# Another order for one period of a recurrent-attention stage: scans a unit and a half ahead, state scan and router steps before the scaling of k, results turned back one period sooner

## The chip, the cores and the metric

The kernel runs on one core of a Trainium2 chip. The metric is the device time of one execution in microseconds; lower is better. Five engines work side by side, each through its own instruction queue in program order: PE (TensorE, matmuls and transposes into PSUM), DVE (VectorE), ACT (ScalarE), POOL (GpSimd) and SP (SyncE, which here issues loads). Instructions of different engines wait for each other through semaphores.

## What is computed

Three operators in a row, all in float32. First a recurrent attention over 4 batches, 8 heads, 768 tokens and 48 dimensions per head. Then a mixture of experts, where a router picks one of 8 experts for each of the 3072 rows. Then a dense feed-forward layer with a squared ReLU. The change touches the first operator and the router.

```python
for t in range(S):                                     # attention
    cur = einsum('bhd,bhe->bhde', u[None] * k_t, v_t)
    y[:, :, t] = einsum('bhd,bhde->bhe', r_t, state + cur)
    state = w_t[:, :, :, None] * state + einsum('bhd,bhe->bhde', k_t, v_t)
...
logits = x @ w_gate                                    # router
e_idx = argmax(logits, axis=1)
gate_w = softmax(logits)[arange(N), e_idx]
eom = sigmoid(x @ w_output_gate)
out[mask] = gate_w * eom * (relu(x[mask] @ w1[e]) @ w2[e])   # for every expert e
...
g = maximum(x @ w_in, 0.0) ** 2                        # dense layer
return g @ w_out
```

## The kernel before, in words

**Units.** The attention is cut into 16 units (`NU`), each one batch and two heads. A unit has 6 chunks of 128 tokens, and the chunks are worked in a parallel form: products inside a chunk, a state that is carried over the chunks, and products with that state. Class `Unit` (from L656) has one method for each stage. The stages of a unit, with the engine that carries each, are these.

- `w_turn` (PE, 6 transposes into two PSUM tiles `zw`), `w_check` (ACT, three instructions), `suffix` and `prefix` for the halves 0 and 1 (DVE: two running products `suf` and `ff` and a reciprocal for each half), `spread` (ACT, copies into `P`).
- `k_turn` and `r_turn`: 12 small transposes each on PE, then two DVE multiplications each, which write `kT` and `rA`. The text calls them the scaling of k and of r.
- `scores` for the halves 0 and 1: 12 matmuls on PE, two ACT copies into `A`, a mask on POOL (L741).
- `k_back` (12 transposes of `kT`, two ACT copies into `kP`), `states` (24 small matmuls), `state_scan` (DVE, writes `St`, L753).
- `gate_products` (POOL, L716 and L717), `gate_sum` (DVE, L721), `gate_values` (POOL, L724, writes `gv`), `bonus_in` (PE, 6 transposes of `gv` that open the output tiles `py`).
- `across` (20 matmuls with `St`) and `within` (24 matmuls with `A`), both adding into `py`; then two ACT copies of `py` into `xT`; `back` (12 transposes of `xT`, two ACT copies into the rows `xr`).

**The period.** The loop `for t in range(-1, NU + 1)` writes the program out by hand: one turn of it is a period, with stages of neighbouring units interleaved. Since every engine works in program order, the order of the calls in this loop is the order of the work on each engine. In period t the kernel before runs, in this order: scores half 0 of unit t, `back` of t-2, `bonus_in` of t-1, `w_turn` of t+2, `gate_sum` and `gate_values` of t, `w_check` of t+2, `k_back` of t, suffix half 0 of t+2, `k_turn` of t+1, `across` of t-1, `spread` of t+1, prefix half 0 of t+2, `r_turn` of t+1, scores half 1 of t, `gate_products` of t+1, suffix and prefix half 1 of t+2, `within` of t-1, `states` and `state_scan` of t.

**PSUM tiles.** `Ring` hands out four PSUM tiles in turn (three named `pt`, one `pa`) to all turns, scores, states and router steps. Each request reuses the tile of four requests before, and PE waits until that one has been read.

**The router's steps.** When the 4 units of a batch are done, `route_steps` (from L160) routes its 768 rows. It is a generator; each `yield` ends a step, and the table `PLAN` (for batches 0 and 1) or `LAST` (batch 2) says at which place of which period a step is issued. Step 1 is the logits on PE (12 matmuls of 256 columns, each issued as two) and an ACT copy `lt`; step 2 turns them back (`lg`); step 3 is the choice of the expert on DVE (L184 to L195, with an exponential `ez` on ACT); step 4 the second part (L198 to L204, with `sg` on ACT); then come the gate weights (L208 to L213), the two counting matmuls `pk` (L220, L221), the row numbers (L227 to L236), and six indirect stores of rows by POOL (L249), one step each.

**Behind the attention.** Batch 3 is routed while the first block of expert 0 (block A, rows of batches 0 to 2) is made ready: `rows_A`, `gather` (POOL), `scale` and `prep_x`, then `up(0)`, its first matmul (L348). `first_block_step` places these.

## Time and profile before

| | |
|---|---|
| median of 3 runs | 855.87 us (854.1 to 857.66) |
| the profiled execution | 851.45 us |
| its span, first to last instruction | 849.7 us |
| PE busy | 809.0 us (95%), 5868 matmuls |
| DVE busy | 532.1 us (63%) |
| ACT busy, POOL busy | 376.1 us (44%), 352.3 us (41%) |
| mean granted TensorE clock | 0.982 of full speed |

The span is one profiled execution; the 1.75 us around it belong to its time and not to the trace. "Busy" of PE counts overlapping records of pipelined matmuls, so 95% is not 95% of what PE can do. The attention lies between 0 and about 187 us; block A's first matmul starts at 190.47 us. In the timeline rows below, a bracket at the end of a row is the time its engine stood idle before it, and what it waited for.

### The profile page before, as it was taken

What the parts mean: (1) busy time and instruction counts of PE and PEld (TensorE: products, weight loads), DVE (VectorE), ACT (ScalarE), POOL (GpSimd) and SP (SyncE); (2) the same over time, 40 slices, a digit from 0 to 9 for tenths busy, and PEclk for the clock granted to TensorE, in tenths of its full rate; (3) what the DMA queues carried; (4) which work ended last, traced back from release to release, by engine and by line L of the source; (5) the groups of instructions that cost most, each with busy time, mean ns of one, the idle gap of its engine ahead of it and who ended that gap; (6) DMA issues with size and microseconds to landing.
All of it is one profiled execution on the core that took longest, in us unless ns stands there. A gap on an engine that the chain in (4) does not pass through costs nothing.

```text
span 849.7 us, 15473 instructions
## 1 busy us (share of the span) xinstructions
PE 809.0 (95%) x5868; PEld 732.2 (86%) x5868; DVE 532.1 (63%) x961; ACT 376.1 (44%) x789; POOL 352.3 (41%) x433
## 2 busy tenths in 40 slices
PE   5998989898899999999999999999999999999995
PEld 4887878778788999999999998888898999999994
DVE  7879787877367778777823688878633434434342
ACT  4565555552354454555544344343433333333321
POOL 6664766653345365455564233333211212123111
PEclk9899999999999999999999999999999999999998
DMA  9575565723596578477762231323204123032010
GB/s 199 112 140 117 138 125 125 222 80 133 132 201 200 172 210 237 130 247 210 169 192 80 79 114 53 128 75 111 75 1 140 31 82 112 2 109 76 1 47 37
DMA packets 157363, 102.89 MB, mean 121 GB/s; under 512 B 112348, under 2 KB 140940, under 8 KB 157284
## 3 DMA queue, kind: packets, MB, share of 16 engines
q1 hardware_dynamic: 149044, 86.55, 38.8%
q0 software_dynamic: 4912, 14.65, 5.0%
q10 hardware_dynamic: 3328, 0.66, 0.4%
q8 instruction: 47, 0.77, 0.4%
q14 instruction: 32, 0.26, 0.1%
HBM read 79.34 MB, written 22.50 MB: 120 GB/s over the span
## 4 chain that ended last, share of the span: by engine, by line
PE 58%; issue 12%; POOL 3%; another core or an unknown queue 0%; DVE 0%; ACT 0%; POOLq 0%; DVEq 0%; ACTq 0%
PE ph L348 10%; PE ph L349 10%; PE ph L350 10%; PE po L348 5%; PE po L350 5%; PE po L349 5%; PE px L350 5%; PE px L348 5%; PE px L349 4%; POOL out_dram L1186 2%; PE px L434 1%; PE po L434 0%; POOL x22l L343 0%; POOL x21l L343 0%; POOL x20l L343 0%
## 5 line engine op out<-in xcount | busy, mean ns | idle before, releaser
L1161 DVE SCALAR_TENSOR_TENSOR gg<-ph,rl 128x512 f32<-128x512 f32 x96 | 66.2, 689 | 121.8 <-ACT rl L1159 115.4
L1159 ACT ACTIVATE rl<-ph 128x512 f32<-128x512 f32 x96 | 57.4, 598 | 146.6 <-PE ph L350 135.5
L343 DVE TENSOR_TENSOR gl<-gg,gh 128x512 fp32r<-128x512 f32 x96 | 66.7, 695 | 65.9 <-ACT gh L341 39.2
L341 ACT CAST gh<-gg 128x512 fp32r<-128x512 f32 x96 | 59.6, 621 | 103.3 <-DVE gg L1161 103.3
L343 POOL TENSOR_TENSOR w1l<-w1r,w1h 128x384 fp32r<-128x384 f32 x56 | 59.5, 1067 | 67.0 <-ACT w1h L341 66.7
L337 ACT ACTIVATE hh<-ph 128x320 fp32r<-128x320 f32 (+7 forms) x64 | 32.4, 507 | 113.2 <-PE ph L350 106.0
L1107 POOL TENSOR_TENSOR caf<-caf,cbf 128x384 f32<-128x384 f32 x32 | 32.5, 1017 | 114.0 <-DVE cbf L1106 114.0
L343 DVE TENSOR_TENSOR w2l<-w2r,w2h 128x384 fp32r<-128x384 f32 x64 | 63.7, 998 | 20.1 <-ACT w2h L341 19.1
L338 DVE SCALAR_TENSOR_TENSOR hl<-ph,hh 128x320 fp32r<-128x320 f32 (+7 forms) x64 | 36.8, 575 | 37.1 <-ACT hh L337 33.0
L1186 POOL DMA_INDIRECT out_dram<-ob,tokc x24 | 23.4, 975 | 66.9 <-DVE ob L1184 64.8
L741 POOL TENSOR_SCALAR_AFFINE_SELECT A<-A 128x768 f32<-128x768 f32 x32 | 27.8, 868 | 45.4 <-ACT A L740 44.9
L348 PE MATMUL po<-hh,w2h 128*128 128x320 f32 (+4 forms) x120 | 42.3, 352 | 0.0
L349 PE MATMUL po<-hl,w2h 128*128 128x320 f32 (+4 forms) x120 | 41.4, 345 | 0.3 <-DVE hl L338 0.3
L350 PE MATMUL po<-hh,w2l 128*128 128x320 f32 (+4 forms) x120 | 41.2, 344 | 0.0
L343 POOL TENSOR_TENSOR x22l<-x2r,x22h 128x512 fp32r<-128x512 f32 x12 | 15.5, 1294 | 51.8 <-ACT x22h L341 51.8
L740 ACT COPY A<-pt 128x384 f32<-128x384 f32 x50 | 22.2, 482 | 32.6 <-PE pt L738 26.0
L738 PE MATMUL pt<-rA,kT 64*128 64x128 f32 x300 | 33.2, 304 | 2.0 <-DVE rA L711 1.4
L404 POOL DMA_INDIRECT xg<-x_rows,gi x28 | 29.0, 1035 | 14.9 <-DVE hl L338 8.5
L343 POOL TENSOR_TENSOR x21l<-x2r,x21h 128x512 fp32r<-128x512 f32 x12 | 15.5, 1291 | 45.5 <-ACT x21h L341 45.5
L341 ACT CAST w2h<-w2r 128x384 fp32r<-128x384 f32 x64 | 32.9, 516 | 0.0
L341 ACT CAST w1h<-w1r 128x384 fp32r<-128x384 f32 x64 | 32.6, 512 | 0.0
L249 POOL DMA_INDIRECT x_rows<-xr,dsi x24 | 24.4, 1018 | 18.8 <-DVE vals L242 14.8
(851 smaller groups left out, 2656.4 us busy)
## 6 DMA issues: line engine op xcount, KB each, us to landing
w1r<-in_moe_w_dram SPq DMA_DIRECT2D x16, 768.0 KB
w2r<-in_moe_w_dram SPq DMA_DIRECT2D x16, 768.0 KB
x2r<-x_cols SPq DMA_DIRECT2D x12, 768.0 KB
cq<-in_moe_w_in_dram SPq DMA_DIRECT2D x16, 384.0 KB
cq<-in_moe_w_out_dram SPq DMA_DIRECT2D x16, 384.0 KB
vN<-in_v_dram SPq DMA_DIRECT2D x32, 144.0 KB
part<-ob SPq DMA_DIRECT2D x24, 192.0 KB
ob<-part SPq DMA_DIRECT2D x24, 192.0 KB
```

Source lines behind the costliest of these rows:

```text
L337: nc.scalar.activation(hi, src, AF.Relu)
L338: nc.vector.scalar_tensor_tensor(lo, src, 0.0, hi.bitcast(F32), op0=ALU.max, op1=ALU.subtract)
L341: nc.scalar.copy(hi, src)
L343: lo_eng.tensor_tensor(lo, src, hi.bitcast(F32), op=ALU.subtract)
L348: nc.tensor.matmul(out_, a_of(ah), b_of(bh), start=start, stop=False)
L349: nc.tensor.matmul(out_, a_of(ah), b_of(bl), start=False, stop=False)
L350: nc.tensor.matmul(out_, a_of(al), b_of(bh), start=False, stop=stop)
L738: nc.tensor.matmul(pa[j][:, ci], self.kT[pp, hf * HC + ci], self.rA[pp, hf * HC + ci], start=True, stop=True)
L1107: nc.gpsimd.tensor_tensor(af, af, bf, op=ALU.add)
L1159: nc.scalar.activation(rl, ph, AF.Relu)
L1161: nc.vector.scalar_tensor_tensor(gg, ph, 0.0, rl, op0=ALU.max, op1=ALU.mult)
L1186: ins = nc.gpsimd.indirect_dma_start(out=out[:, :], out_offset=IndirectOffsetOnAxis(ap=tokc[:, n:n + 1], axis=0), in_=ob, in_offset=None)
```

## The change

It changes the order of one period, and little else. In period t the order is now: scores half 0 of unit t, `k_back` of t, `w_check` of t+2, `gate_products` of t+1, suffix and prefix half 1 of **t+1**, `within` of t-1, `states` and `state_scan` of t, the router's steps of the place "scan", scores half 1 of t, `spread` of t+1, `across` of t-1, `k_turn` and `r_turn` of t+1, `w_turn` of t+2, `bonus_in` of **t**, `gate_sum` and `gate_values` of **t+1**, suffix and prefix half 0 of t+2, and `back` of **t-1**. The scans thus run one and a half units ahead (before: two units), and only unit 0's first half is scanned before the loop. `within` stands before `across`, so the copies of `py` into `xT` follow `across`. The router's counting matmuls stand before the gate weights, with an ACT copy of their result for batches 0 to 2, and the steps have other places. Line numbers of the changed file are 4 smaller from there on.

```diff
 (route_steps)
-        if b < B - 1:
-            gate_weights()
-            yield
         pk = ps_t.tile([128, 512], F32, name=pn)
...
         nc.tensor.matmul(pkv[:, :, :NTB], upper[:, 0], oh, start=False, stop=True)
+        if b < B - 1:
+            nc.scalar.copy(inc, pkv)
+            pkv = inc
         yield
-        if b == B - 1:
-            gate_weights()
-            yield
+        nc.vector.tensor_reduce(sg[:, 0], ez.rearrange("p e t -> p t e"), axis=AX.X, op=ALU.add)
...
+        nc.vector.tensor_copy(xr[:, :, DM:], tail[:, b])
+        yield
 (tables)
-        PLAN = ((5, "turned"), (5, "across"), (5, "late"), (6, "gate"), (6, "across"), (7, "turned"), (7, "turned"),
-                (7, "across"), (7, "mask1"), (8, "turned"), (8, "across"), (8, "mask1"), (9, "turned"))
-        LAST = ((5, "turned"), (5, "across"), (5, "late"), (6, "gate"), (6, "scans"), (6, "scans"), (6, "scans"),
-                (6, "across"), (6, "mask1"), (6, "late"), (6, "late"), (7, "turned"), (7, "turned"))
+        PLAN = ((4, "gate"), (5, "back"), (5, "scan"), (5, "scan"), (6, "back"), (6, "scan"), (7, "scan"),
+                (7, "turned"), (7, "gate"), (8, "back"), (8, "turned"), (9, "back"), (9, "turned"))
+        LAST = ((4, "gate"), (5, "back"), (5, "scan"), (5, "scan"), (5, "turned"), (5, "gate"), (6, "scan"),
+                (6, "scan"), (6, "turned"), (6, "gate"), (6, "end"), (7, "back"), (7, "scan"))
 (the loop, as it is now)
+            at(t, "scores", 0)
+            at(t, "k_back")
+            at(t + 2, "w_check")
+            step(t, "back")
+            first_block_step(t, "back")
+            if t + 1 < NU - 1:
+                at(t + 1, "gate_products")
+            at(t + 1, "suffix", 1, z)
+            at(t + 1, "prefix", 1, z)
+            at(t - 1, "within")
+            at(t, "states")
+            at(t, "state_scan")
+            step(t, "scan")
+            at(t, "scores", 1)
+            at(t + 1, "spread")
+            at(t - 1, "across")
+            at(t + 1, "k_turn")
+            at(t + 1, "r_turn")
+            step(t, "turned")
+            first_block_step(t, "turned")
+            at(t + 2, "w_turn")
+            at(t, "bonus_in")
+            if t + 1 == NU - 1:
+                at(t + 1, "gate_products")
+            at(t + 1, "gate_sum")
+            at(t + 1, "gate_values")
+            at(t + 2, "suffix", 0)
+            at(t + 2, "prefix", 0)
+            step(t, "gate")
+            first_block_step(t, "gate")
+            if t < NU:
+                at(t - 1, "back")
+            step(t, "end")
```

In `first_block_step` the pieces of block A move with the places: `rows_A` to the start of period 15, `gather` to its end, `scale` to the start of period 16, and the first part of batch 3's logits behind `across` of unit 15.

The order on DVE, batch 0's routing, before (`St_146` is the state scan of unit 5, `mx` to `inc` the router's steps 3 and 4, `g` the gate sum, `suf` a half scan of unit 8, `kT` the scaling of k of unit 7):

```order
L753 SCALAR_TENSOR_TENSOR St_146<-pa,P_149 128x288
L184 TENSOR_REDUCE mx<-lg 128x6
L186 TENSOR_TENSOR z<-lg,mx 128x48
L190 SCALAR_TENSOR_TENSOR cand<-z,e_228 128x48
L192 TENSOR_REDUCE m_1296<-cand 128x6
L195 TENSOR_TENSOR oh_72<-cand,m_1296 128x8x6
L721 TENSOR_REDUCE g<-g_1252 128x12
L198 TENSOR_TENSOR zo<-lg,oh_72 128x48
L200 TENSOR_REDUCE zs<-zo 128x6
L204 SCALAR_TENSOR_TENSOR inc<-rst,oh_72 128x56
L691 SCALAR_TENSOR_TENSOR suf<-zw,s_142 128x388
L706 TENSOR_TENSOR kT<-pt,suf 128x6x64
```

and now (`kT` is that of unit 6):

```order
L749 SCALAR_TENSOR_TENSOR St_146<-pt,P_149 128x288
L184 TENSOR_REDUCE mx<-lg 128x6
L186 TENSOR_TENSOR z<-lg,mx 128x48
L190 SCALAR_TENSOR_TENSOR cand<-z,e_219 128x48
L192 TENSOR_REDUCE m_1222<-cand 128x6
L195 TENSOR_TENSOR oh_72<-cand,m_1222 128x8x6
L198 TENSOR_TENSOR zo<-lg,oh_72 128x48
L200 TENSOR_REDUCE zs<-zo 128x6
L204 SCALAR_TENSOR_TENSOR inc<-rst,oh_72 128x56
L702 TENSOR_TENSOR kT<-pt,suf 128x6x64 x2
```

Steps 3 and 4 now stand together right behind the state scan, with no scan between them and the scaling of k; the gate weights, which followed a few instructions later in the same period, stand one period on.

The same place on ACT, before (`A` are the copies of scores, `xT` those of the output, `ez` and `sg` the router's two exponentials):

```order
L178 COPY lg<-pt 128x2x3x16
L740 COPY A_1240<-pt 128x3x128 x2
L781 COPY xT<-py 128x384 x2
L188 ACTIVATE ez<-z 128x48
L740 COPY A_1307<-pt 128x3x128 x2
L785 COPY xr<-pt 128x6x48
L785 COPY xr<-pa 128x6x48
L202 ACTIVATE sg<-zs 128x6
```

and now:

```order
L178 COPY lg<-pt 128x2x3x16
L188 ACTIVATE ez<-z 128x48
L202 ACTIVATE sg<-zs 128x6
L736 COPY A_1234<-pt 128x3x128
L736 COPY A_1234<-pa 128x3x128
L697 COPY P_147<-suf 128x48x5
L777 COPY xT<-py 128x384 x2
L781 COPY xr<-pt 128x6x48 x2
```

Both exponentials, which wait for DVE, now stand ahead of the copies of scores half 1, of `spread` and of the copies into `xT`.

On PE, a plain period before, from scores half 1 to the state matmuls:

```order
L738 MATMUL pt<-rA,kT 128x128 x6
L778 MATMUL py<-A_440,vN_138 64x128 x6
L778 MATMUL py<-A_540,vN_138 64x128 x6
L748 MATMUL pt<-vN_139,f_141 64x48 x2
L748 MATMUL pt<-vN_139,kP 64x48 x10
```

and now, from `k_back` to `across`:

```order
L667 MATMUL pt<-ident,kT 128x64 x12
L765 MATMUL py<-A_319,vN_137 64x128 x6
L765 MATMUL py<-A_371,vN_137 64x128 x6
L744 MATMUL pa<-vN_138,f_141 64x48 x2
L744 MATMUL pa<-vN_138,kP 64x48 x10
L734 MATMUL pt<-rA,kT 128x128 x6
L775 MATMUL py<-rA,St_145 64x128 x10
```

Between `k_back` and the state matmuls that read its copies `kP`, PE now has only `within`; before, `across`, `r_turn` and scores half 1 lay between them as well.

## Rows read from the trace of the kernel before

**Rows 1.** Windows of 20 us: busy us of each engine, granted clock, DMA share, GB/s.

```profile
20.00:40.00 20.00, 19.52 (x292) 17.49 (x290) 16.34 (x28) 11.29 (x26) 11.28 (x10) 0.83 0.62 120
40.00:60.00 20.00, 19.51 (x357) 17.73 (x351) 16.64 (x28) 13.16 (x31) 13.29 (x12) 1.00 0.64 125
...
300.00:320.00 20.00, 20.00 (x108) 19.38 (x107) 14.29 (x22) 10.41 (x25) 11.43 (x11) 1.00 0.76 244
```

**Rows 2.** Timeline of DVE, one plain period: start us, us, engine, line, instruction.

```profile
41.83 0.73 DVE L753 TENSOR_TENSOR_SCAN St<-pt,P 128x288 f32<-128x288 f32 x1
44.13 0.75 DVE L721 TENSOR_REDUCE g<-g 128x12 f32<-128x576 f32 x1 [1.56 <-POOL g L717]
...
48.58 0.96 DVE L691 TENSOR_TENSOR_SCAN suf<-zw,s 128x388 f32<-128x388 f32 x1
...
50.66 0.73 DVE L753 TENSOR_TENSOR_SCAN St<-pa,P 128x288 f32<-128x288 f32 x1
```

**Rows 3.** Timeline of PE at full clock, and the one wait of the period above.

```profile
51.45 0.27 PE L671 MATMUL pa<-ident,xT 64*128 64x64 f32 x1 [0.26 <-DVE St L753]
...
67.03 1.01 PE L738 MATMUL pt<-rA,kT 64*128 64x128 f32 x12
...
67.97 1.53 PE L778 MATMUL py<-A,vN 128*64 128x128 f32 x24
69.33 0.27 PE L748 MATMUL pa<-vN,f 128*64 128x48 f32 x4
```

**Rows 4.** Timeline of DVE, the period with batch 0's routing.

```profile
70.25 0.74 DVE L753 TENSOR_TENSOR_SCAN St<-pa,P 128x288 f32<-128x288 f32 x1
...
71.39 1.35 DVE L190 SCALAR_TENSOR_TENSOR cand<-z,e 128x48 f32<-128x48 f32 x1
...
74.57 1.06 DVE L204 TENSOR_TENSOR_SCAN inc<-rst,oh 128x56 f32<-128x56 f32 x1
...
78.39 0.21 DVE L208 TENSOR_REDUCE sg<-ez 128x6 f32<-128x48 f32 x1
...
80.12 1.01 DVE L711 TENSOR_TENSOR rA<-pt,ff 128x384 f32<-128x384 f32 x2
...
83.13 0.73 DVE L753 TENSOR_TENSOR_SCAN St<-pt,P 128x288 f32<-128x288 f32 x1
```

**Rows 5.** Timeline of POOL in that period.

```profile
71.27 1.42 POOL L717 TENSOR_TENSOR g<-g,u_bc 128x576 f32<-128x576 f32 x1
```

**Rows 6.** Timeline of DVE, the same router steps for batch 3.

```profile
189.96 0.23 DVE L184 TENSOR_REDUCE mx<-lg 128x6 f32<-128x48 f32 x1
...
190.46 0.21 DVE L190 SCALAR_TENSOR_TENSOR cand<-z,e 128x48 f32<-128x48 f32 x1
...
191.62 0.26 DVE L204 TENSOR_TENSOR_SCAN inc<-rst,oh 128x56 f32<-128x56 f32 x1
```

**Rows 7.** Timeline of PE, a wait for the copies of `k_back` in batch 1's routing.

```profile
121.45 0.27 PE L671 MATMUL pa<-ident,rN 64*128 64x64 f32 x1 [1.56 <-ACT kP L730]
```

**Rows 8.** Windows of 1.5 us around batch 0's routing, same columns as rows 1.

```profile
82.00:83.50 1.50, 0.55 (x11) 0.36 (x7) 1.43 (x4) 0.86 (x2) 1.05 (x1) 1.00 0.78 156
...
85.00:86.50 1.50, 1.50 (x9) 1.50 (x9) 1.24 (x8) 1.47 (x3) 0.00 (x0) 0.50 0.39 79
```

**Rows 9.** Timelines of the start: DVE, POOL, PE.

```profile
8.40 0.96 DVE L697 TENSOR_TENSOR_SCAN ff<-zw,f 128x387 f32<-128x387 f32 x1
...
11.70 1.40 POOL L717 TENSOR_TENSOR g<-g,u_bc 128x576 f32<-128x576 f32 x1
...
22.68 0.58 PE L738 MATMUL pa<-rA,kT 64*128 64x128 f32 x1
```

**Rows 10.** Timeline of PE, the last unit's first scores to block A.

```profile
171.79 0.94 PE L738 MATMUL pt<-rA,kT 64*128 64x128 f32 x12
...
180.98 1.50 PE L169 MATMUL pt<-xT,wcat 128*32 128x256 f32 x18
...
190.47 0.42 PE L348 MATMUL ph<-x0h,w1h 128*128 128x320 f32 x1
```

More of the change, by code (lines that the diff above doesn't have):

```diff
@@ L763, in bonus_in, with within @@
                                      start=ci == 0, stop=False, skip_group_check=True)
+            def within(self):
+                for c in range(NC):
+                    hf, ci = divmod(c, HC)
+                    for j in range(2):
+                        nc.tensor.matmul(self.py[hf][64 * j:64 * j + 64, ci], self.vN[:, c, j], self.A[hf][:, ci, j], start=False, stop=c == 0,
+                                         skip_group_check=True)
             def across(self):
+                if self.pr == 0:
+                    xTs[self.b] = rw.tile([128, HP, S], F32, name="xT")
                 for c in range(1, NC):
@@ L769, in across @@
                         pp = slice(64 * j, 64 * j + 64)
-                        nc.tensor.matmul(self.py[hf][pp, ci], self.St[pp, :, c], self.rA[pp, c], start=False, stop=False, skip_group_check=True)
-            def within(self):
-                if self.pr == 0:
-                    xTs[self.b] = rw.tile([128, HP, S], F32, name="xT")
-                for c in range(NC):
-                    hf, ci = divmod(c, HC)
-                    for j in range(2):
-                        nc.tensor.matmul(self.py[hf][64 * j:64 * j + 64, ci], self.vN[:, c, j], self.A[hf][:, ci, j], start=False, stop=True,
-                                         skip_group_check=True)
+                        nc.tensor.matmul(self.py[hf][pp, ci], self.St[pp, :, c], self.rA[pp, c], start=False, stop=True, skip_group_check=True)
                 for hf in range(2):
@@ L819, in first_block_step @@
                 blkA.w1r, blkA.w2r = ({hf: words[hf][q] for hf in range(2)} for q in range(2))
-            if NU - 2 <= t < NU and place == "casts":
+            if NU - 2 <= t < NU and place == "back":
                 for f in range(2 * (t - NU + 2), 2 * (t - NU + 2) + 2):
                     first["A"].prep_w(f, nc.vector, part="hi")
-            if (t, place) == (NU - 1, "scans"):
+            if (t, place) == (NU - 1, "back"):
                 rows_A(rw)
-            if t == NU - 1 and place == "late":
+            if t == NU - 1 and place == "turned":
                 for f in range(FA):
                     first["A"].prep_w(f, nc.vector, part="lo")
+            if t == NU - 1 and place == "gate":
                 first["A"].gather()
+            if t == NU and place == "back":
+                first["A"].scale(nc.vector)
             if t == NU and place == "turned":
@@ L831, in first_block_step @@
                 route_step()
-            if t == NU and place == "late":
-                first["A"].scale(nc.vector)
         setup_first()
-        at(0, "w_turn")
-        at(1, "w_turn", first_z)
-        for hf in range(2):
-            at(0, "suffix", hf)
-            at(0, "prefix", hf)
+        at(0, "w_turn", first_z)
+        at(0, "suffix", 0, first_z)
+        at(0, "prefix", 0, first_z)
         at(0, "w_check")
@@ L851, in rwkv_moe_kernel @@
             at(t, "scores", 0)
-            at(t - 2, "back")
-            step(t, "turned")
-            first_block_step(t, "turned")
-            at(t - 1, "bonus_in")
-            if t >= 0:
-                at(t + 2, "w_turn")
-            at(t, "gate_sum")
-            at(t, "gate_values")
-            step(t, "gate")
-            at(t + 2, "w_check")
-            at(t, "k_back")
-            if t >= 0:
-                at(t + 2, "suffix", 0)
-            at(t + 1, "k_turn")
-            step(t, "scans")
-            first_block_step(t, "scans")
-            at(t - 1, "across")
-            at(t + 1, "spread")
-            first_block_step(t, "casts")
-            if t >= 0:
-                at(t + 2, "prefix", 0)
-            step(t, "across")
-            at(t + 1, "r_turn")
-            at(t, "scores", 1)
-            step(t, "mask1")
-            at(t + 1, "gate_products")
-            if t == -1:
-                at(1, "suffix", 0, z)
-                at(1, "prefix", 0, z)
-            at(t + 2, "suffix", 1, z)
-            at(t + 2, "prefix", 1, z)
+            at(t, "k_back")
+            at(t + 2, "w_check")
+            step(t, "back")
[4 more added lines that the diff above has]
+            at(t + 1, "prefix", 1, z)
             at(t - 1, "within")
```

17 lines of the change are left out of this document (6 added, 11 removed).

## The prediction, made before the changed kernel was timed

> **What bounds the kernel now.** I read the windows first. Behind the attention PE is busy in all of a 20 us window at full clock [rows 1], and each block's work waits for routing, which waits for the attention. So what the attention stage saves or loses should reach the end of the kernel one to one, and only that stage has to be costed. Inside it PE is busy 19.51 of 20 us in a stretch without router steps, DVE 16.64.
>
> Then I read a plain period on DVE. From one state scan to the next it takes 50.66 - 41.83 = 8.83 us, with one idle gap of 1.56 us before the gate sum [rows 2]; DVE's own work is thus 7.27 us. PE waits 0.26 us in that period [rows 3], so its work is about 8.55 us. Plain periods are bound by PE, and an order of work can gain almost nothing there.
>
> Periods with the router are another matter. In batch 0's the state scans stand at 70.25 and 83.13, 12.9 us apart, and DVE is never idle between them [rows 4]: steps 3, 4 and the gate weights all fall into one period. There DVE sets the pace and PE waits. Behind it PE works at half clock: granted 1.00 at 82 us with 0.55 us busy of 1.5, then 0.50 at 85 us with PE full [rows 8]. So the gain to be had is at the start, in three routing periods, and at the end.
>
> **A plain period after the change.** I walk it by hand with the rows' durations; time 0 is the start of scores half 0. PE: scores 0.94 us (67.03 to 67.97), `within` 1.36 us (67.97 to 69.33) [rows 3]; `across`, the transposes, the second scores and the state matmuls are the rest of the 8.55. Scores end at 0.9. `k_back` needs the PSUM tiles that ACT empties for `back`, whose copies end at about 1.0, so it waits some 0.2 us and ends at 1.55. `within` covers the copies of scores and of `kP` and ends at 2.9; the state matmuls wait perhaps 0.1 and end at 3.9. Second scores end at 4.8, `across` at 6.15, the turns of k and r at 7.0, `w_turn` at 7.75, `bonus_in` at 8.45, `back` at 8.9. The next scores need `rA`: k's turn is done at 6.6, and two pairs of multiplications at about 0.95 us each (a pair is listed as 1.01 [rows 4]) plus a quarter microsecond give 8.75. That just fits. So **a plain period is 8.9 us**, 0.1 longer than now. DVE has 7.27 us to do in it, so about 1.5 us stay idle before the scaling of k. This is where the router's steps go.
>
> **The routing periods.** For one batch, four periods.
>
> - The first issues the logits: 18 of the 24 matmuls are listed with 1.50 us [rows 10], so 24 take 2.0 us, all on PE: 8.9 + 2.0 = 10.9.
> - The second has steps 3 and 4 between the state scan and the scaling of k. Where POOL is quiet they take 1.92 us, from 189.96 to the end of `inc` at 191.88 [rows 6]. In batch 0's period they took some 4.0 us: 70.9, where the scan hands over, to 75.6, less 0.7 for the gate sum between them [rows 2, 4]. The difference lies in single operations: `cand` took 1.35 us, starting at 71.39 within POOL's 1.42 us product that began at 71.27 [rows 4, 5], and 0.21 us alone [rows 6]. In the new order POOL's products end at about 5.75 and the mask of scores half 1 can't start before its copies, which ACT holds behind `sg`. So the steps run from 5.4 with POOL quiet, and I take 1.92; 4.0 is the other end. Then ACT: `sg` at 7.2, two copies of scores to 8.1, `spread` to 8.65, copies into `xT` to 9.5. `r_turn` waits for the first, `bonus_in` and `back` for the last. PE ends at 10.4 instead of 8.9. DVE alone would allow 9.4, so the queue on ACT is late next. **10.4 us**, or 12.5 with the long steps.
> - The third has the counting matmuls, some 0.55 us of PE, and the gate weights, 78.39 to 80.12 or 1.73 us on DVE at most [rows 4], against 1.5 of slack: 9.45.
> - The fourth has row numbers on DVE, under the slack, and row stores on POOL, which has time: 9.0.
>
> Their sum is 39.75 us. The third batch has counting matmuls and gate weights in its second period too, and I take 11.2 us for that one.
>
> The Trainium skill, "SBUF — State Buffer", section "Who interferes with whom", says that a VectorE instruction with two SBUF inputs blocks against a GpSimd instruction that reads SBUF, and that the later one waits for the whole of the earlier. The 1.35 against 0.21 us agrees. By that rule the 1.92 us hold only while POOL stands idle; an instruction of POOL's that is under way when the steps begin makes the time that of the first rival below.
>
> **The start.** DVE ends unit 0's scans at 9.3, as now [rows 9], and goes straight to its scaling (to 11.15). Then the gate sum of unit 0 waits for POOL's product, which ends at 13.1 [rows 9]; two half scans follow at 2.08 us each (48.58 to 50.66 [rows 2]), the state scan at 18.1, unit 1's scaling to 20.7. Unit 1's first scores start at about 21.0, against 22.68 [rows 9]. PE at that point has also turned unit 0's bonus, which comes later in the order before.
>
> **The end.** From the last unit's first scores PE has, at full clock, 6.9 us to the end of `bonus_in`, then `back` of unit 14 to 7.85, `within` to 9.2, `across` to 10.55, the logits' 2.0 us to 12.6, and block A's turns, step 2 and the last `back` to 15.0. Now it is 190.47 - 171.79 = 18.7 us [rows 10].
>
> **The sum.** First scores of unit 1 at 21.0; periods 1 to 3 at 8.9, and 2.5 us for the low clock at the start (the window from 20 to 40 us was granted 0.83 [rows 1], or 3.4 us of 20, and I take most of that), 29.2; two batches 79.5; periods 12 to 14 as 10.9 + 11.2 + 9.0 = 31.1. So the last unit starts at 160.8 and its 14 periods took 139.8 us, next to 171.79 - 22.68 = 149.1 now [rows 9, 10]. Block A starts at 175.8 instead of 190.47. That is 14.7 us. A walk by hand forgets small waits, and plain periods now show 0.26 us of them [rows 3], so I give 0.2 us for each of 16 periods back, 3 us. **The forecast is 11.7 us less**, 839.8 for the profiled execution's 851.45. The median of the runs is 855.87, 4.4 above that execution; I set the difference against the median: **844 us**, or between 839 and 849 if the small waits are none or twice as many and the routing periods come within a microsecond.
>
> **The rivals.**
>
> *The router's steps stay long and the clock falls again.* Steps 3 and 4 meet POOL's products, at 4.0 us; the second period is 12.5. PE then waits some 3.5 us and the half clock of rows 8 returns, worth about 2 us for each batch. Each batch then costs 2.1 + 2 = 4.1 us more than in the sum, 12.3 for three, and the 11.7 us are gone: 856, no change. For it: DVE reaches the steps later if the half scans slip. Against: `sg` on ACT keeps POOL's mask away. The skill's "TensorE: Matmul & The Clock Gate", section "HAM oscillation", warns of just such gaps between bursts; that PE falls to half clock behind DVE-bound stretches the windows agree.
>
> *The state matmuls wait for `kP` in every period: slower.* Place: between `k_back` and `states` only `within` is left as cover, where before `across`, `r_turn` and second scores stood there too. If ACT is behind with the copies, PE stands. Price: PE has waited 1.56 us for these copies once [rows 7]; 16 of that are 25 us, and 855.87 - 11.7 + 25 = 869. It decides from 11.7 / 16 = 0.73 us per period on. Against: my walk has the copies done at 2.8 and `within` at 2.9, and ACT is busy 13.16 of 20 us [rows 1].
>
> *It does more.* With no small waits and no half clock early, 14.7 + 2.5 us come off: 838.7, or a little less.
>
> **How the numbers follow.** 0.5% of the median, 4.3 us, is about what a measurement of this kernel can tell from no change: 851.6 to 860.2. Forecast 0.70, long steps 0.16, `kP` wait 0.07, more 0.07. Faster: the forecast, the last case and, where only one of its two halves comes (long steps without the clock, 850), 0.04 of the long steps: 0.81. Same: the other 0.12 of them. Slower: 0.07. The range from 837 to 853 leaves out that 0.12, the 0.07 of the `kP` wait and a little of the last case, together about 0.2.
>
> **What would show it.** Right: state scans 8.9 apart in plain periods, DVE idle 1.5 us before k's scaling with PE as the releaser, 10 to 11 us in the period with steps 3 and 4, `cand` near 0.2 us, granted clock 1.00 from about 27 us to 170, block A's first matmul at 176 to 180. Wrong: plain periods of 9.5 or more with PE waiting for `kP` or for `rA`, `cand` at 1.3 us, or clock windows of 0.50 behind the routing periods.

## The result, and the profile after

| | before | after |
|---|---|---|
| median of 4 runs each | 855.01 us (854.1 to 857.66) | 848.12 us (842.87 to 848.6) |
| ratio, 95% interval | | 0.990 (0.9855 to 0.9946) |
| the profiled execution, its span | 851.45, 849.7 us | 848.16, 846.3 us |
| last unit's first scores | 171.79 us [rows 10] | 162.73 us |
| block A's first matmul | 190.47 us [rows 10] | 183.31 us |

The change makes the kernel 6.9 us faster. The forecast was 844, the range 837 to 853; of the 11.7 us forecast as gain, somewhat more than half came. Run again beside other kernels (below) the changed kernel took 844.45 us (12 runs), with a ratio of 0.9952 (0.993 to 0.9975). The kernel before had medians between 849.7 and 856.6 us there, from one set of runs to the next; each set (experiments 1 to 4, 5 to 8, 9 to 12) ran on another chip. So runs of different sets are compared below by their ratios to before, or by their profiles. The changed kernel itself ran in the set of 5 to 8 alone, and its two ratios, 0.990 and 0.9952, lie so far apart that for the other sets a small gain or loss against it is read from profiles and not from times.

**Windows** of the changed kernel, columns as in [rows 1]:

```profile
20.00:40.00 20.00, 19.98 (x311) 18.19 (x307) 16.01 (x28) 11.30 (x26) 11.29 (x10) 1.00 0.61 120
40.00:60.00 20.00, 19.97 (x350) 17.51 (x351) 17.31 (x30) 12.77 (x31) 12.47 (x12) 1.00 0.72 141
...
100.00:120.00 20.00, 17.86 (x281) 16.11 (x276) 15.91 (x33) 11.66 (x30) 12.61 (x18) 0.91 0.55 122
...
140.00:160.00 20.00, 17.93 (x280) 15.99 (x274) 16.85 (x40) 12.18 (x32) 11.10 (x20) 0.91 0.70 219
```

PE is full from 20 to 60 us, and the clock is 1.00 where [rows 1] had 0.83. (The trace's record of the clock starts at 24.0 us here. Matmuls of the scores up to 23.8 us still took 0.42 us each, against 0.27 later, so the first of these microseconds were at half clock too.) In two later windows PE is busy two microseconds less, and the clock is down.

**A plain period** on DVE, which answers to [rows 2]:

```profile
44.90 0.73 DVE L749 TENSOR_TENSOR_SCAN St<-pt,P 128x288 f32<-128x288 f32 x1
46.80 1.02 DVE L702 TENSOR_TENSOR kT<-pt,suf 128x384 f32<-128x384 f32 x2 [1.18 <-PE pt L667]
...
53.48 0.73 DVE L749 TENSOR_TENSOR_SCAN St<-pt,P 128x288 f32<-128x288 f32 x1
```

8.58 us from scan to scan, where before had 8.83. DVE's one gap ends on PE's turn of k, as forecast; it is 1.18 us long, where the forecast had 1.5.

**Periods of steps 3 and 4**, batch 0 and then batch 1, on DVE; they answer to [rows 4]:

```profile
63.55 0.76 DVE L749 TENSOR_TENSOR_SCAN St<-pt,P 128x288 f32<-128x288 f32 x1 [1.41 <-PE pt L744]
...
64.48 0.67 DVE L186 TENSOR_TENSOR z<-lg,mx 128x48 f32<-128x48 f32 x1
65.18 0.21 DVE L190 SCALAR_TENSOR_TENSOR cand<-z,e 128x48 f32<-128x48 f32 x1
...
66.34 0.27 DVE L204 TENSOR_TENSOR_SCAN inc<-rst,oh 128x56 f32<-128x56 f32 x1
...
74.27 0.76 DVE L749 TENSOR_TENSOR_SCAN St<-pa,P 128x288 f32<-128x288 f32 x1 [0.41 <-PE pa L744]
...
102.87 0.76 DVE L749 TENSOR_TENSOR_SCAN St<-pt,P 128x288 f32<-128x288 f32 x1 [1.24 <-PE pt L744]
...
103.80 0.47 DVE L186 TENSOR_TENSOR z<-lg,mx 128x48 f32<-128x48 f32 x1
104.30 1.44 DVE L190 SCALAR_TENSOR_TENSOR cand<-z,e 128x48 f32<-128x48 f32 x1
...
115.98 0.76 DVE L749 TENSOR_TENSOR_SCAN St<-pt,P 128x288 f32<-128x288 f32 x1 [1.78 <-PE pt L744]
```

Batch 0's is 10.72 us long, near the forecast's 10.4; batch 1's is 13.11, and batch 2's (144.92 to 158.09) 13.17. The others are 9.3 to 10.1. From `mx` to `inc` the steps took 2.4 us in batch 0 and 3.4 us in batch 1, where the forecast had 1.92. The cause of this first microsecond is on POOL. These are its rows from batch 0's and from batch 1's period:

```profile
63.68 1.41 POOL L713 TENSOR_TENSOR g<-g,u_bc 128x576 f32<-128x576 f32 x1
...
101.69 1.01 POOL L245 DMA_INDIRECT x_rows<-xr,dsi  x1 [0.16 <-issue]
...
102.77 1.42 POOL L712 TENSOR_TENSOR g<-kN,rN 128x576 f32<-128x576 f32 x1
104.26 1.41 POOL L713 TENSOR_TENSOR g<-g,u_bc 128x576 f32<-128x576 f32 x1
```

In batch 0 `z`, one step earlier, lasts until the second product ends (0.67 us; in batch 3, with POOL idle, 0.21), and `cand` begins behind it. In batch 1 a row store of batch 0 (place "back") stands ahead of the two products, and the second lies over `cand`: 1.44 us, not 0.21. The rest is ACT's queue and the clock, on PE's timeline (batch 0, then batch 1) and in windows of 1.5 us (batch 1):

```profile
67.08 0.27 PE L667 MATMUL pt<-ident,rN 64*128 64x64 f32 x1 [0.93 <-ACT A L736]
...
107.42 0.97 PE L667 MATMUL pt<-ident,rN 64*128 64x64 f32 x12 [1.95 <-ACT A L736]
```

```profile
105.50:107.00 1.50, 0.00 (x0) 0.00 (x0) 1.36 (x7) 0.20 (x2) 0.28 (x3) 1.00 0.03 10
...
110.00:111.50 1.50, 1.50 (x20) 1.33 (x20) 1.43 (x4) 0.40 (x2) 1.15 (x1) 0.50 0.75 191
```

`r_turn` waits for the copies of scores, which stand behind `sg` on ACT. PE does nothing for 1.5 us and works at half clock 3 us later, as in [rows 8].

**The tail**, POOL, DVE and PE, beside [rows 10]:

```profile
171.21 1.09 POOL L245 DMA_INDIRECT x_rows<-xr,dsi  x1 [0.22 <-issue]
172.30 0.89 POOL L737 TENSOR_SCALAR_AFFINE_SELECT A<-A 128x768 f32<-128x768 f32 x1
...
174.81 0.99 POOL L400 DMA_INDIRECT xg<-x_rows,gA  x1 [1.61 <-DVE w2l L339]
```

```profile
177.95 0.51 DVE L411 TENSOR_SCALAR xg<-xg 128x384 f32<-128x384 f32 x1 [3.40 <-DMA xg<-x_rows,gA]
```

```profile
173.24 0.88 PE L765 MATMUL py<-A,vN 128*64 128x128 f32 x12 [2.37 <-POOL bia L920]
174.05 2.40 PE L775 MATMUL py<-rA,St 64*64 64x128 f32 x20
...
183.31 0.41 PE L344 MATMUL ph<-x0h,w1h 128*128 128x320 f32 x1
```

The mask of the last half unit comes at 172.30, behind two row stores of batch 2; PE waits 2.37 us for it, and `across` then takes 2.40 us, where it took 1.40 in other periods. The gather of block A's rows starts only when the stores have landed. Its bracket names a DVE instruction, but the semaphore records of the trace have POOL's queue waiting for the last stores: the last one landed at 174.03, and the gather started 0.78 us later. It is 0.78 to 0.79 us in eleven of the fourteen profiles; in the others (before, experiments 7 and 8) the last mask stands in between, and it is 0.9 to 1.5. DVE and PE then wait for the gathered rows. From the last unit's first scores to block A it is 20.6 us; the forecast gave 15.0, and before it was 18.7.

### The profile page after: what moved, and what is told of

It reads as the page before. It is cut to its first block, busy times and chain, and to the rows that moved or that the text cites. A ratio compares the mean times of both kernels' runs of the same rounds, so it can differ in the third digit from the quotient of the medians.

```text
span 846.3 us, 15487 instructions
## 1 busy us (share of the span) xinstructions
PE 808.7 (96%) x5868; PEld 733.0 (87%) x5868; DVE 533.8 (63%) x961; ACT 374.6 (44%) x792; POOL 351.9 (42%) x433
## 4 chain that ended last, share of the span: by engine, by line
PE 69%; issue 13%; DVE 8%; POOL 4%; DMA 4%; ACT 1%; POOLq 0%; DVEq 0%; SPq 0%; ACTq 0%
PE ph L345 9%; PE ph L344 9%; PE ph L346 9%; PE po L344 5%; PE px L344 5%; PE px L346 5%; PE po L346 5%; PE po L345 5%; PE px L345 5%; POOL out_dram L1177 2%; PE py L765 2%; PE pt L667 2%; PE pt L734 2%; DMA xg<-x_rows,gi 2%; DMA x_rows<-xr,dsi 2%
## 5 line engine op out<-in xcount | busy, mean ns | idle before, releaser
L333 ACT ACTIVATE hh<-ph 128x320 fp32r<-128x320 f32 (+7 forms) x64 | 32.5, 508 | 112.9 <-PE ph L346 104.1
L339 POOL TENSOR_TENSOR x20l<-x2r,x20h 128x512 fp32r<-128x512 f32 x12 | 15.5, 1292 | 35.9 <-ACT x20h L337 35.9
```

The costliest lines, as they stand in the source:

```text
L333: nc.scalar.activation(hi, src, AF.Relu)
L339: lo_eng.tensor_tensor(lo, src, hi.bitcast(F32), op=ALU.subtract)
```

## The experiments

In all of them the numbers named "first scores" and "block A" are the last unit's first scores and block A's first matmul in the profiled execution. "Destinations" are the row numbers that the row stores use.

**1. Row stores and destinations of batch 2 sooner.**

```diff
-        LAST = ((4, "gate"), (5, "back"), (5, "scan"), (5, "scan"), (5, "turned"), (5, "gate"), (6, "scan"),
-                (6, "scan"), (6, "turned"), (6, "gate"), (6, "end"), (7, "back"), (7, "scan"))
+        LAST = ((4, "gate"), (5, "back"), (5, "scan"), (5, "scan"), (5, "turned"), (5, "gate"), (6, "back"),
+                (6, "back"), (6, "scan"), (6, "turned"), (6, "turned"), (6, "gate"), (7, "back"))
```

> Changed kernel with batch 2's destinations and its six row stores a place or two earlier, so that the last store stands ahead of the mask of the last unit's first half and none between the two masks. Theory (GpSimd's row stores ahead of the last mask hold TensorE, and the idle TensorE then runs at the half clock): the 2.37 us wait of within for GpSimd in the last unit goes, across takes 1.4 us as elsewhere and not 2.40, the 24 logits about 1.4 us and not 2.50; the logits of batch 3 come at about 172.5 instead of 176.38, the gather of block A about 2 us sooner, block A's first matmul at about 180.5 instead of 183.31; the time falls by 2 to 4 us, to about 845. Rival (the gather's landing is the bound of the tail whatever the masks do): the logits come sooner but block A starts within 1 us of 183.31, and the time stays within 1.5 us of 848.1.

843.39 us, ratio 0.9898 (0.9864 to 0.9933). The last store does not stand ahead of both masks, as the expectation has it, but between them (masks at 169.02 and 171.14, the store at 170.10). The wait for the mask went and the logits took 1.93 us at full clock, but they came at 177.87, later than either theory had. Block A came at 182.77, as the rival has it. The destinations now stand ahead of unit 15's half scans on DVE, and the two periods there are 14.2 and 12.7 us long (13.2 and 9.8 in the first profile). Block A followed the last store by 12.7 us. The edit moved two things; experiment 7 moves the stores alone.

**2. Row stores behind the gate products.**

```diff
-                (7, "turned"), (7, "gate"), (8, "back"), (8, "turned"), (9, "back"), (9, "turned"))
+                (7, "turned"), (7, "gate"), (8, "scan"), (8, "turned"), (9, "scan"), (9, "turned"))
```

> Changed kernel with batch 0's and batch 1's row stores of the place in front of the gate products moved behind them. Theory (that store pushes GpSimd's second product into the router's steps, and the step cand then takes 1.44 us and not 0.21, which makes the periods of steps 3 and 4 of batches 1 and 2 long): cand is 0.2 in all three batches, these two periods fall from 13.11 and 13.17 to about 10.7 as in batch 0, the last unit's first scores come at about 158 instead of 162.73, and the time falls by 3 to 5 us. Rival (ScalarE's queue makes them long: the copies of the scores stand behind the router's two exponentials): cand is short, but TensorE's wait for the score copies stays over 1 us and the half clock returns; the periods stay over 12 us, and the last scores come within 2.5 us of 162.73.

841.28 us, ratio 0.9892 (0.9856 to 0.9928). POOL and DVE in batch 1:

```profile
101.36 1.41 POOL L712 TENSOR_TENSOR g<-kN,rN 128x576 f32<-128x576 f32 x1
102.85 1.41 POOL L713 TENSOR_TENSOR g<-g,u_bc 128x576 f32<-128x576 f32 x1
104.19 0.09 POOL L805 MEMSET bia<- 1x1 f32 x1
104.44 1.01 POOL L245 DMA_INDIRECT x_rows<-xr,dsi  x1 [0.16 <-issue]
```

`cand` is 0.21 in all batches, the two long periods fall to 10.58 and 11.63, the waits of `r_turn` to 0.80 and 0.81, the clock stays at 1.00 through these periods, and first scores come at 158.64. In this profile the theory holds to within a microsecond. Block A comes at 180.36: of the 4.1 us won at the first scores 1.1 are lost again in the tail.

**3. The two exponentials behind ACT's copies.**

```diff
-            step(t, "scan")
             at(t, "scores", 1)
             at(t + 1, "spread")
             at(t - 1, "across")
+            step(t, "scan")
```

> Changed kernel with the router's steps issued behind the second half's scores, the spread and the output copies: VectorE's and TensorE's orders are the same, only ScalarE's two exponentials stand behind its score, spread and output copies (and GpSimd's small fills and stores behind a mask). Theory (ScalarE's queue): the waits of r's turn for the score copies (0.93, 1.95 and 1.94 us) go, TensorE stays at full clock through the periods of steps 3 and 4, which fall from 10.72, 13.11 and 13.17 to about 10, 11 and 11 though cand stays at 1.4 in the last two; the last unit's first scores at about 158, the time down by 3 to 5 us. Rival (VectorE's steps set these periods): VectorE's work of 10.8 us stays, TensorE's wait moves from r's turn to the scores (for rA), the clock falls all the same, and the periods are within 0.7 us of before.

842.92 us, ratio 0.9905 (0.9872 to 0.9939). ACT in batch 1:

```profile
102.40 0.86 ACT L736 COPY A<-pt 128x384 f32<-128x384 f32 x2 [0.72 <-PE pt L734]
...
104.40 0.28 ACT L188 ACTIVATE ez<-z 128x48 f32<-128x48 f32 x1
```

`r_turn` no longer waits, the periods are 9.96, 10.60 and 12.41, and first scores come at 158.55, though `cand` still takes 1.32 us in batches 1 and 2. So VectorE's long step and ScalarE's queue are two conditions of one loss: without either, `r_turn`'s wait is short or gone and the clock stays up. It is not PE's wait as such: in batch 2 PE waited 1.84 us here, for DVE ahead of the counting matmuls, and the clock didn't fall.

**4. State scan and router steps behind k's scale again.** `states`, `state_scan` and `step(t, "scan")` moved behind `k_turn`.

> Changed kernel with one part undone: state matmuls, state scan and the router's steps of a period again behind k's turn and scale. Theory (the state scan in front of k's scale is what brought the gain): plain periods go from 8.58 back to 8.8 or more, periods with router steps to 12 or more because r's scale waits for the steps and k's scale no longer covers them; the last unit's first scores at about 168 to 171, and the time is back at 853 or more. Rival (the gain is the other placing of the router's steps within the batch, and VectorE's slack of about 1.5 us a period hides the order): the last scores within 2.5 us of 162.73 and the time within 2 us of 848.1.

849.30 us, ratio 0.9984 (0.9963 to 1.0005), no clear gain over the kernel before left. Plain periods are 8.88, as the theory has it; the steps' periods are 10.9, 10.9 and 11.7, below it, with `cand` at 0.21. First scores at 164.72 fit the rival. Block A, at 187.74, is 4.4 us later than in the first profile: 2.0 of them are there at the first scores, and 2.4 come in the tail, where batch 2's destinations now wait for k's scale, the first row store starts at 163.54 and the last at 173.87. Each theory has half.

**5. The changed kernel again.**

> The changed kernel itself once more, as the measure for the runs beside it. Theory (its time depends on whether the last gather of expert block 1 meets the next weights in the DMA queues: block A's first matmul plus 659 us is the span where it doesn't, as in the kernel before and in three of the trials, plus 663 us in the profiled execution of the changed kernel, where it did): single times lie in two groups some 4 to 5 us apart, and a profile with the weights issued 0.3 us behind the gather is of the slower group. Rival (the spread of the single times has no place in the program): times spread evenly, and the profile's span less block A's first matmul is 659 in any case.

844.45 us (843.35 to 846.78), and the times show no two groups 4 to 5 us apart: as put, the theory falls. So does the rival's second half, that the span less block A's first matmul is 659 us in any case (below). The profile differs from the first one of the same program in two places. PE waits as long in batches 1 and 2, but the clock doesn't fall:

```profile
107.88 0.96 PE L667 MATMUL pt<-ident,rN 64*128 64x64 f32 x12 [1.88 <-ACT A L736]
```

```profile
110.00:111.50 1.50, 1.50 (x28) 1.28 (x26) 1.47 (x3) 0.64 (x2) 1.21 (x2) 1.00 0.43 88
```

The periods are 11.35 and 12.38, 1.8 and 0.8 us below the 13.1 and 13.2 of the first; that difference I take to be the half clock's, in the main. And the last gather of expert block 1's rows wasn't late. Here are the first execution's rows on POOL, SP and DVE, and the second's on POOL and SP:

```profile
211.29 0.93 POOL L400 DMA_INDIRECT xg<-x_rows,gi  x1 [0.30 <-issue]
```

```profile
211.62 0.41 SPq L324 DMA_DIRECT2D w1r<-in_moe_w_dram  x1
```

```profile
221.52 0.42 DVE L411 TENSOR_SCALAR xg<-xg 96x384 f32<-96x384 f32 x1 [7.95 <-DMA xg<-x_rows,gi]
```

```profile
210.95 0.94 POOL L400 DMA_INDIRECT xg<-x_rows,gi  x1 [0.30 <-issue]
...
213.99 0.41 SPq L324 DMA_DIRECT2D w1r<-in_moe_w_dram  x1
```

In the first, the next weights are issued 0.33 us behind the gather, its rows come 10 us after its issue, and PE waits 5.87 us. In the second the weights follow 3.04 us later, and PE doesn't wait. Span less block A's first matmul is 663.0 us in the first, 658.4 in the second, 659.2 before.

**6. Those weights later.** `blocks[1].load(1)` and `convert_load(0)` moved behind `put_A(0)`.

> Changed kernel with expert block 1's second half of weights and the first conversion load issued behind block A's first output store on SyncE, some 2 to 3 us later. Theory (1.5 MB of weights ahead of or among the packets of the last gather of expert block 1 make it land 10 us after its issue): that gather lands within 3 us, TensorE's wait of 5.87 us at expert block 1's turns falls below 2 us, and the time is that of the faster group of the changed kernel in every run, 3 to 5 us under the slower group. Rival (the gather is late for another reason, its own chain of row stores): the wait stays, and the time is that of the changed kernel beside it within 1.5 us.

847.25 us, ratio 0.9990 (0.9970 to 1.0010): 2.8 us slower than the changed kernel beside it. The gather was in time, but it was so in experiment 5 too. DVE now stood 5.4 us before the first conversion of `cq` (weights of the dense layer), whose load I had moved along, and PE waited 3.68 us for `hl` (a part of the hidden rows that DVE makes) at 239.25. The edit exchanged one late transfer for another and doesn't decide between the theories.

**7. Batch 2's row stores sooner, and nothing else.**

```diff
-                (6, "scan"), (6, "turned"), (6, "gate"), (6, "end"), (7, "back"), (7, "scan"))
+                (6, "scan"), (6, "turned"), (6, "turned"), (6, "gate"), (6, "end"), (6, "end"))
```

> Changed kernel in which batch 2's destinations stay where they are and only row stores two to six stand sooner: two of them ahead of the gate's bonus of the last unit, all of them ahead of its two masks. Theory (block A starts 12 to 14 us after the start of batch 2's last row store, as in all six profiles so far, so that GpSimd's stores set the tail): the last store starts at about 169 instead of 171.21, block A's first matmul at about 181 instead of 183.31, and the time is 1.5 to 2.5 us under that of the changed kernel beside it. Rival (the last unit's masks and TensorE set it): masks come no sooner, the last logits stay at about 176, and block A starts within 0.7 us of 183.31.

840.76 us, ratio 0.9914 (0.989 to 0.9938), 3.7 us under the changed kernel beside it: more than the theory has. The last store started at 169.33, as it says. But logits at 176.55 fit the rival, and block A at 182.36 lies between the two. That profile is of the slowest of seven executions (845.28), in which the clock had fallen in both long periods (12.73 and 12.76 us), so it doesn't show where the 3.7 us of the median come from. From last store to block A it is 13.0 us again, but here PE went straight from the logits to the gathered rows, without a wait for them:

```profile
176.55 2.83 PE L169 MATMUL pt<-xT,wcat 128*32 128x256 f32 x24
179.32 1.21 PE L430 MATMUL pt<-ident,xg 128*128 128x128 f32 x6
```

**8. All three** (2, 3 and 7 together).

> Changed kernel with three edits of the trials together: row stores behind the gate products, the router's exponentials behind ScalarE's copies, batch 2's row stores sooner as in the run beside it. Theory (each takes away another part: GpSimd's products beside the step cand, ScalarE's queue, GpSimd's stores in the tail): periods of steps 3 and 4 at 9.9, 10.0 and 11.0 or less, last unit's first scores at about 156.5 instead of 162.73, block A's first matmul at about 176.5, the time 5 to 8 us under that of the changed kernel beside it. Rival (the first two edits take away the same wait, and the third gains nothing once the gather's landing is the bound): first scores at about 158, block A at about 180, the time no better than 841.3 of the run with the stores moved alone.

837.89 us, ratio 0.9882 (0.9857 to 0.9908), 6.6 us under the changed kernel. The time fits the theory, and so do the first two periods (9.97 and 9.97, but 11.77 for the third, where it has 11.0); first scores at 159.14 are nearer to the rival, block A at 178.69 lies between. In 7 and 8 the copies of the last half unit's scores started late, at 171.08 and 166.49 (2.93 and 2.51 us idle ahead of them on ACT), and PE waited 2.7 and 2.8 us in `bonus_in`. With the last store behind the first mask, experiment 12, that wait is gone. The late copies also hold the last mask and with it the gather. Why they are held there stays open.

**9. Results turned back a period later, as before.**

```diff
             at(t, "scores", 0)
+            at(t - 2, "back")
...
-            if t < NU:
-                at(t - 1, "back")
```

> Changed kernel with another part undone: the results of a unit turned back a period later, behind the first scores of a period, as in the kernel before. Theory (this part is worth something in the tail only, where one unit instead of two is left to turn back): the plain period stays at 8.6, the last unit's first scores within 1 us of those of the changed kernel (161.3 to 162.7), block A's first matmul 0.5 to 1 us later, the time within 1.5 us of the changed kernel's 844.45. Rival (the two result copies stand ahead of the score copies on ScalarE and of k's turn back on TensorE, and hold the state matmuls): every period 0.3 us longer, the last scores 4 us later, the time 4 us longer.

853.19 us, ratio 0.9955 (0.9929 to 0.9981). The rival, and in plain periods by more than it had: they are 9.42 us instead of 8.58. First scores come at 164.96 (2.2 to 3.7 later than in the two profiles of the changed kernel), block A at 186.93. PE's work is the same, but a window shows it waiting, and DVE's gap before k's scale is longer:

```profile
40.00:60.00 20.00, 19.05 (x325) 16.68 (x328) 15.91 (x26) 12.01 (x28) 11.78 (x11) 1.00 0.66 128
```

```profile
47.44 1.02 DVE L702 TENSOR_TENSOR kT<-pt,suf 128x384 f32<-128x384 f32 x2 [1.88 <-PE pt L667]
```

From the order of the calls I read a loop through two engines: scores, `k_back`, `within`, `states`, scores half 1, `across` and `k_turn` on PE, then two scalings of about a microsecond each on DVE, then scores again. While DVE scales, PE can only do what isn't part of the loop: `r_turn`, `w_turn`, `bonus_in` and, in the changed order, `back`. With `back` behind the scores it lies inside the loop.

**10. The router in one period for batches 0 and 1.**

```diff
-        PLAN = ((4, "gate"), (5, "back"), (5, "scan"), (5, "scan"), (6, "back"), (6, "scan"), (7, "scan"),
+        PLAN = ((4, "gate"), (5, "back"), (5, "scan"), (5, "scan"), (5, "turned"), (5, "gate"), (6, "scan"),
```

> Changed kernel with batch 0's and batch 1's counting matmuls and gate weights in the period of steps 3 and 4, and their destinations a period sooner, as it stands for batch 2. Theory (VectorE's and TensorE's work is the same, only the period it falls in differs): the period of steps 3 and 4 grows from 10.7 to about 12 (batch 0) and from 11.4 to about 12.6 (batch 1), the two periods behind it fall by about 0.5 each, the last unit's first scores come 0.5 to 1.5 us later, the time rises by 0 to 1.5 us. Rival (the spread over periods keeps TensorE from idling): TensorE's waits pass 2 us, the clock falls to its half in both periods, these take 13 us or more and the time rises by 4 us.

847.18 us, ratio 0.9876 (0.9836 to 0.9915). The steps' period is 12.95 and 13.13, the one behind it 8.54 and 10.31, the next 8.32 and 8.72; first scores at 162.94. These two are longer than the theory has (12 and 12.6), but `r_turn`'s waits (0.92 and 1.94 us) stay at the first profile's, below the rival's 2 us, and first scores are 0.2 us later than there. What one period loses the next ones give back: over the three of batch 0 it is 29.8 us against 29.7. The spread of these steps isn't where the gain lies.

**11. More work on DVE.** A reduction behind every state scan:

```diff
+            def more(self):
+                nc.vector.tensor_reduce(self.g, self.vN[:, :, :, :D], axis=AX.X, op=ALU.add)
...
             at(t, "state_scan")
+            at(t, "more")
```

> Changed kernel with one more reduction on VectorE behind every state scan, of 576 elements a row into a buffer that nothing reads any more, about 0.74 us each, 16 in all. Theory (TensorE sets the plain period, VectorE has 1.2 us of idle time ahead of k's scale): plain periods stay at 8.6 to 8.7, the wait of k's scale falls from 1.2 to about 0.45, and only the periods with router steps grow, by up to 0.74 each: the last unit's first scores 2 to 5 us later, the time 2 to 5 us longer. Rival (the chain from the state scan over k's and r's scale to the scores is what sets the period): every period grows by 0.74, plain ones to 9.3, the last scores come 11 us later and the time rises by 9 us or more.

848.24 us, ratio 0.9888 (0.9844 to 0.9931). Plain periods stay at 8.58, and the gap before k's scale shrinks from 1.18 us to this:

```profile
46.60 1.02 DVE L702 TENSOR_TENSOR kT<-pt,suf 128x384 f32<-128x384 f32 x2 [0.54 <-PE pt L667]
```

So DVE has slack there, as the prediction said. First scores at 163.56 are 0.8 later than in the first profile and 2.3 later than in experiment 5's. In the steps' periods of batches 1 and 2 the added work moved `z` under the product, and `z` took 1.27 and 1.28 us, `cand` 0.21; `r_turn` waited 2.19 us both times, and the periods were 13.56 and 12.66. From this I read that what counts is how late `sg` comes, whichever step the product holds.

**12. The best version**: 2 and 3, and five of batch 2's six stores ahead of both masks.

```diff
-                (6, "scan"), (6, "turned"), (6, "gate"), (6, "end"), (7, "back"), (7, "scan"))
+                (6, "scan"), (6, "turned"), (6, "turned"), (6, "gate"), (6, "end"), (7, "back"))
```

> The three edits together once more, with batch 2's last row store between the masks of the last unit's two halves (five of the six stand ahead of both). Theory (in the run of all three, the copies of the last unit's second half of scores started at 166.49, behind GpSimd's last store, and TensorE then waited 2.81 us and fell to the half clock): with that store behind the first mask the copies come at about 164, the wait of bonus_in falls below 1.5 us, block A's first matmul comes at about 177.5 instead of 178.69, and the time is 836 to 837.5. Rival (the landing of the row stores and the gather set block A's start, 12 to 14 us behind the start of the last store): the last store starts about 0.8 us later, block A at 179 or more, and the time is 838 or more.

840.92 us where before took 856.64, ratio 0.9808 (0.9774 to 0.9842). Its profile fits the theory, and is a little earlier than that has it: the copies of the last half unit's scores start at 161.01, PE lists no wait ahead of `bonus_in`, and

```profile
163.62 1.08 POOL L245 DMA_INDIRECT x_rows<-xr,dsi  x1 [0.18 <-issue]
```

```profile
176.65 0.63 PE L344 MATMUL ph<-x0h,w1h 128*128 128x320 f32 x1
```

First scores came at 156.57. The time that the expectation names held for the profiled execution (837.29) and not for the median. Against the kernel before this is the best ratio of all, 1.9% less time. But the kernel before was slowest in this set, and experiment 8, on another chip, had the lower median (837.89); these runs don't tell which of the two is faster. Both beat the kernel before, and experiment 8 the changed kernel in its own set.

## Why the prediction came out as it did

- **The number** lies in the range, but by luck in part. From 14.7 us at block A in the sum the start takes 2.0 and the tail 5.6, which leaves 7.1; 7.2 were measured. The 3 us given back for small waits in every period were never lost as such; they covered part of the start's and the tail's errors.
- **Plain period**: 8.9 forecast, 8.58 measured. That PE bounds it and DVE has slack is shown by experiment 11. But "an order of work can gain almost nothing there" was wrong as reasoning: experiment 9 loses 0.84 us a period by order alone, and its rows fit that PE's waits depend on what stands in the gap of DVE's scalings. `k_back`'s 0.2 us and the other small waits of the walk weren't there; PE never waited for `kP` in a plain period, and the slower rival fell.
- **Router periods**: 10.4 forecast for steps 3 and 4 (11.2 for batch 2, with the counting matmuls); 10.72, 13.11 and 13.17 measured. **The step that failed is "the steps run from 5.4 with POOL quiet"**: it was walked for batch 0 alone, and not quite kept there either, since the same walk lets POOL's products end at 5.75. In batch 0 the steps took 2.4 us and not 1.92 (`z`). From batch 1 on POOL has a row store of the batch before ahead of its products (experiment 2), and they took 3.4. The first rival came half true, with its `cand` and its half clock, in two batches of three. The forecast did name ACT's queue as late next, but as 10.4 us and not as a cause of the half clock (experiment 3).
- The Trainium skill's rule ("SBUF — State Buffer", section "Who interferes with whom") is borne out: `cand` took 1.30 to 1.44 us in every period in which a product lay over it, and 0.21 in all others.
- **14 periods**: 139.8 us forecast, 162.73 - 22.96 = 139.8 measured. The agreement is of errors that cancel. Counted from first scores to first scores, periods 1 to 3 took 26.0 us against 29.2: plain periods are shorter, and the 2.5 us set aside for the low clock were hardly needed (full clock from 24 us on, before from 27). Batch 0's four periods took 39.5 against 39.75, batch 1's 41.7 against 39.75, and batch 2's three 32.5 against 31.1.
- **The start**: 21.0 forecast, 22.96 measured, 2.0 short. The state scan stood at 17.95, as forecast (18.1). Then PE's turn of k waited 1.25 us for it, because `Ring` gives that turn the tile of the state matmuls, and PE's turns ran at half clock.
- **The tail: 15.0 forecast, 20.6 measured, the largest error.** "PE has, at full clock, 6.9 us ..., then ..." counted PE's work alone and put POOL's queue at nothing. When the logits start, 3.1 of the 5.6 us are there: the wait for the mask behind POOL's stores, and the half clock after it. The rest comes behind them, with PE at half clock and waiting for the gathered rows. The change left six stores, two masks and a bonus product on POOL. In all fourteen profiles block A starts 12.1 to 14.3 us behind the start of batch 2's last row store. In eleven PE waits for the gathered rows; in experiments 1, 7 and 8 it doesn't and comes late itself, so POOL's stores bound the tail in most profiles and not in all. Experiment 7 shows that moving the stores alone is worth 3.7 us.
- **One to one to the end**: block A gains 190.47 - 183.31 = 7.2 us, the forecast had 11.7. In the first profile 3.8 of these are lost again at expert block 1, in experiment 5's none. The rows say where (a gather behind which weights are issued at once); that the weights delay it is argued, not shown. PE waited 3.8 to 7.0 us for those rows in four profiles, all with the weights 0.3 to 1.1 us behind the gather; of the others, two with 0.7 and 1.2 us had no such wait, nor had any with 2.9 us or more.

What brought the gain: the state scan and router steps ahead of k's scale (undone in experiment 4, where no clear gain is left: periods of 8.88 us and batch 2's destinations late) and `back` in the gap of the scalings (undone in experiment 9, which is 6.0 us slower than experiment 10 of the same set; its profile has the late gather too, with a wait of 7.0 us, so not all of the 6.0 need be the order's). Neither set has the changed kernel beside it. That scans run a unit and a half ahead wasn't tried alone, nor `within` ahead of `across`.

## What to carry to other kernels

Follow a hand-written period over all its turns, not one: a queue that is quiet in the first batch carries the stores of the first batch in the second. For a stage's end, ask which queue the next stage's data comes out of; here it was in most profiles POOL's row stores, and not the engine that bounds the periods. Where two engines pass work around in a loop, put what is outside the loop into the gap in which the other one works; the sum of the work doesn't show it.

## What was not expected of the hardware

- The clock fell behind short waits, and not always. In periods with steps 3 and 4 PE waited 1.8 to 2.2 us for ACT's copies in 14 cases (seven profiles), and the windows behind show a fall in 11 of them; with waits of 0.8 to 1.3 us it fell in none of 12. The same program with 1.95 and 1.88 us fell once and didn't once. Two waits there for DVE, 1.84 us (experiment 3) and 2.34 us (experiment 4), were followed by no fall.
- DVE's splits `w1l` and `w2l` took 1.51 and 1.77 us beside POOL's stores and masks in the tail (168.54 and 171.85 us), 0.54 to 0.55 us each for their neighbours.
- The kernel before had medians from 849.7 to 856.6 us in four sets of runs, as much as the whole gain of this change; each of the later three sets was on another chip, and only comparisons within a set told the versions apart.
